# Sparse attention and MLP on one core: the softmax chain moved into one step, its normalization on ScalarE, its splitting on GpSimd

## The chip, the core and the metric

The kernel runs on one core of a Trainium2 chip. The core has five engines with a queue of instructions each, worked off strictly in order: TensorE (PE in the profile, with PEld for its weight loads), VectorE (DVE), ScalarE (ACT), GpSimd (POOL) and SyncE (SP), which here only issues DMAs. The engines wait for each other by semaphores. The metric is the device time of one execution in microseconds (us), lower is better. The kernel before takes 1460.08 us, the median of three runs from 1459.34 to 1460.13.

## The reference

Attention that keeps the 32 largest scores of each row, and then a two-layer MLP with a leaky ReLU, all in float32:

```python
# q, k, v: (8 batches, 8 heads, 576 rows, 64)
scores = q @ k.T / sqrt(64)                       # (8, 8, 576, 576)
kth = np.partition(scores, -32, axis=-1)[..., -32:-31]
scores = np.where(scores >= kth, scores, -1e9)
attn = np.exp(scores - scores.max(-1, keepdims=True))
attn = attn / (attn.sum(-1, keepdims=True) + 1e-9)
x = (attn @ v).transpose(0, 2, 1, 3).reshape(4608, 512)
h = x @ w_in                                      # w_in: 512 x 2048, in float64
out = np.maximum(0.01 * h, h) @ w_out             # w_out: 2048 x 512, in float64
```

## The kernel before, in words

**Units and steps.** The attention is cut into 144 *units*. Nearly every unit is 128 query rows of one pair of heads, so its scores are a tile of 128 partitions by 2 x 576 float32 (`s_sb`, held by `u.both` and `u.s`, five buffers); a few units per batch join the 64 left-over rows of two pairs. The main loop (L653 to L717) makes one pass per unit, called a *step* here. In step s, VectorE runs the top k of unit s, and the other engines work on units before and after it. All instructions are recorded in the order in which the loop writes them (`manual_schedule`), so the order on each engine's queue is that of the text.

**The chain of one unit**, with the step in which each part stands in the code before, for unit n:

- Step n-2 or so: `scores` (L218) on TensorE, for two units at once in every even step; four copies by ScalarE bring them from PSUM into `s_sb` (L242).
- Step n: `top_k` (L299) on VectorE, in four rounds, each of which is one `slot()` of the step: the halves of the row are paired by max and min (L306), and each round finds the eight largest (`MAX8`, L311) and strikes them out (`MATCH_REPLACE8`, L314).
- Step n+1: `limits` (L318) on GpSimd (three small instructions: `nleast`, then `nbias` twice), `mask` (L328, two ScalarE activations), `exponents` (L332, two more, which also give the sums), and `sums` (L336, `ze` on ScalarE), the last of them near the end of the step.
- Step n+2: `reciprocals` (L340, `rz` on VectorE), `normalize` (L344, two GpSimd multiplications of 128 x 576), and `transpose` (L347): ScalarE copies the upper and the lower 16 bits of all weights into two tiles (`split`, L354), SyncE writes both to DRAM (`apart`, L355) and brings them back through a transposing DMA (`wT`, L359).
- `values` (L635), attention times v on TensorE into a PSUM tile `wide` (L398, L410), for both units of a pair n, n+1 in the same step, and `keep_values` (L417), ScalarE's copies into `x` (L422). `values_at` (L525) says when: for a unit below 14 in the middle of step (n | 1) + 4, and from there on at the end of step (n | 1) + 3 (one step less for three units in `HURRIED`).

For units 14, 15, 23 and 31 (`HASTY`), `transpose_in_haste` (L361) takes the place of the DMAs: nine TensorE transposes into two PSUM tiles `wide`, and two ScalarE copies from there into `wT` (`keep_transposed`, L372).

**The MLP** goes over 19 chunks of tokens: two of 128, then seventeen of 256. A chunk becomes ready when the values of its last unit are kept: chunk 0 after units 0 to 3, chunk 1 after 4 to 7, chunk 2 after 8 to 15, and so on. TensorE does the hidden layer (`ph`, L467; L435 for the first two chunks) and the output layer (`pz`, L479); ScalarE applies the leaky ReLU (L473, L440) and copies the output (L488). `mlp_steps` (L501) puts a piece of this work at seven places in each step, and `slot_budget` (L553) sizes the pieces so that a chunk is used up when the next becomes ready. The last chunk is worked off after the loop (L718).

**What else stands in the order of the first steps.** Weights come in float64 and are turned to float32 first (`round_weights`, L115), until about 60 us. `score_early` (L573) computes the scores of twelve later units at the ends of steps 0 to 5 (4, 2, 1, 2, 1, 2 units): TensorE into `wide` and `narrow` PSUM tiles, two ScalarE copies per unit (L290), and a store to DRAM (`kept`). There are two PSUM tiles `wide`, shared by scores, early scores, transposes and values, and one `narrow`.

The heart of a step in the code before, where `old` is unit s-1 and `older` unit s-2:

```python
limits(old); weights_of(older)     # rz and the two multiplications of unit s-2
mask(old, 0); mask(old, 1)
exponents(old, 0)
transpose(older, lambda: mlp_steps(budget))
exponents(old, 1); sums(old)       # ze of unit s-1, used in step s+1
```

Of the kernel before, what the change touches and what calls it, by code (L numbers as in the profile page):

```python
# [13 lines left out]
AF = mybir.ActivationFunctionType  # L14
ALU = mybir.AluOpType

NKC = 5
# [3 lines left out]
def kernel(  # L21
# [13 lines left out]
    nc = tc.nc  # L35
# [4 lines left out]
    ROUNDS = TOPK // 8  # L40
# [258 lines left out]
    def top_k(u):  # L299

        u.tops = small.tile([P, 2, ROUNDS, 8], F32, name="tops")
        pairs = work.tile([P, 2, 2, HS], F32, name="pairs", bufs=1)
        for n, op in enumerate((ALU.max, ALU.min)):
            nc.vector.tensor_tensor(pairs[:, :, n, :], u.both[:, :, 0:HS], u.both[:, :, HS:S], op)  # L306
        for r in range(ROUNDS):
            rest = [pairs[:, i, 0, :] if r < ROUNDS // 2 else
                    pairs[:, i, :, :].rearrange("p n h -> p (n h)") for i in range(2)]
            for i in range(2):  # L310
                nc.vector.max(out=u.tops[:, i, r, :], in_=rest[i])  # L311
            if r + 1 < ROUNDS:
                for i in range(2):
                    nc.vector.match_replace(out=rest[i], in_to_replace=u.tops[:, i, r, :],  # L314
                                            in_values=rest[i], imm_value=LOWEST)
            yield

    def limits(u):  # L318

        largest, least_kept = u.tops[:, :, 0, 0], u.tops[:, :, ROUNDS - 1, 7]  # L320
        u.nleast = small.tile([P, 2], F32, name="nleast")
        u.nbias = small.tile([P, 2], F32, name="nbias")
        u.z = small.tile([P, 2], F32, name="z")
        nc.gpsimd.tensor_scalar(u.nleast, least_kept, -1.0, None, ALU.mult)  # L324
        nc.gpsimd.tensor_tensor(u.nbias, least_kept, largest, ALU.subtract)  # L325
        nc.gpsimd.tensor_scalar(u.nbias, u.nbias, SCALE, None, ALU.mult)

    def mask(u, i):  # L328

        nc.scalar.activation(u.s[i], u.s[i], AF.Prelu, bias=u.nleast[:, i:i + 1], scale=1.0, alpha=BELOW)  # L330
# [9 lines left out]
    def reciprocals(u):  # L340
        u.rz = small.tile([P, 2], F32, name="rz")
        nc.vector.reciprocal(u.rz, u.ze)  # L342

    def normalize(u, i):  # L344
        nc.gpsimd.tensor_scalar(u.s[i], u.s[i], u.rz[:, i:i + 1], None, ALU.mult)  # L345

    def transpose(u, between):  # L347


        pairs = u.both.rearrange("p i n -> p (i n)").bitcast(U16).rearrange("p (n h) -> p n h", h=2)  # L350
        apart = halves.tile([P, 2, 2 * S], U16, name="apart")
        for h in range(2):
            split = work.tile([P, 2 * S], U16, name="split", bufs=2)
            nc.scalar.copy(split, pairs[:, :, h])  # L354
            nc.sync.dma_start(apart[:, h, :], split)  # L355
            if h == 0:
                between()
        u.wT = work.tile([P, 2 * NKC - 1, P], F32, name="wT", bufs=3)
        nc.sync.dma_start_transpose(out=u.wT.bitcast(U16), in_=apart.rearrange("p h n -> (p h) n"))  # L359

    def transpose_in_haste(u):  # L361

        both = u.both.rearrange("p i n -> p (i n)")
        u.parts_T = []
        for c0, c1 in ((0, 8), (8, 2 * NKC - 1)):
            pt = ps_sc.tile([P, 2, 512], F32, name="wide", bufs=2)
            pt = pt.rearrange("p h (c n) -> p (h c) n", n=P)
            for c in range(c0, c1):
                nc.tensor.transpose(pt[:, c - c0, :], both[:, c * P:(c + 1) * P], ident)
            u.parts_T.append((c0, c1, pt))  # L370
# [18 lines left out]
    def weigh_whole(us, po, order):  # L389

        for m, c in enumerate(order):
            for side in range(2):
                k = slice(side * LEFT, (side + 1) * LEFT) if c == QUARTERS else slice(0, P)
                at = min(c, NKC - 1)
                for n, u in enumerate(us):
                    nc.tensor.matmul(  # L398
                        po[n * D:(n + 1) * D, side, 0:P],
                        v_of[u.pairs[0]][k, at, side, :],  # L400
                        u.wT[k, at + side * NKC if at + 1 < NKC else at, :],
                        start=(m == 0), stop=(m == NKC - 1),
                    )
# [112 lines left out]


    LAG = 3
    HURRY = 20
    HURRIED = (15, 23, 31)  # L520
    HASTY = (14, 15, 23, 31)
    UNHURRIED = 14
    MIDDLE, END = 0, 1

    def values_at(n):  # L525

        if n < UNHURRIED:
            return (n | 1) + LAG + 1, MIDDLE
        return (n | 1) + LAG - ((n | 1) in HURRIED), END

    steps = units

# [3 lines left out]
    def unit(n):  # L536
        return steps[n] if 0 <= n < len(steps) else None
# [26 lines left out]
    with tc.manual_schedule():  # L564
# [62 lines left out]
            if 0 <= n - len(jobs) + HP + 1 < HP:  # L627
                load_qk(n - len(jobs) + HP + 1)

        def weights_of(u):  # L630
            reciprocals(u)
            normalize(u, 0)
            normalize(u, 1)

        def values(*place):  # L635
            due = [u for n, u in enumerate(steps) if values_at(n) == place]
            if not due:
                return ()
            po = ps_sc.tile([P, 2, 512], F32, name="wide", bufs=2)
            if len(due[0].pairs) == 1:  # L640
                weigh_whole(due, po, FULL + [NKC - 1] if place[1] == MIDDLE else
                            [QUARTERS] + FULL if place[0] < HURRY else FULL + [QUARTERS])
                return [(due[0], po[:, :, 0:P])]
            for n, u in enumerate(due):
                weigh_left(u, po[:, :, n * LEFT:(n + 1) * LEFT])
            return [(u, po[:, :, n * LEFT:(n + 1) * LEFT]) for n, u in enumerate(due)]

        def keep(weighed, *place):
            for u, po in weighed:
                keep_values(u.pairs[0], po, u.b, u.q0)  # L650
            attended(*place)

        for s in range(len(steps) + LAG + 1):  # L653
            assert s < 7 or not to_keep
            cur, old, older, new = unit(s), unit(s - 1), unit(s - 2), ()
            if s % 2 == 0:
                new = [u for u in steps[s + 2:s + 4] if u]
            picks = top_k(cur) if cur else iter(())
            budget = slot_budget(s)

            def slot():
                next(picks, None)

            at_first = s < HURRY and s - 2 in HURRIED
            if at_first:
                weights_of(older)
            slot()
            if old:
                limits(old)
            late = s < HURRY and not {s - 1, s - 2} & set(HURRIED)  # L670
            if older and not late and not at_first:
                weights_of(older)
            mlp_steps(budget)
            if old:
                mask(old, 0)
                mask(old, 1)
            weighed = values(s, MIDDLE)
            at_once = s - 2 in HASTY or any(at == (s, MIDDLE) for at, _ in ready_at)
            if at_once:
                keep(weighed, s, MIDDLE)  # L680
            slot()
            if older and late:
                weights_of(older)
            if s - 2 in HASTY:
                transpose_in_haste(older)
            mlp_steps(budget)
            if old:
                exponents(old, 0)
            mlp_steps(budget)
            if older:  # L690
                keep_transposed(older) if s - 2 in HASTY else transpose(older, lambda: mlp_steps(budget))
            if not older or s - 2 in HASTY:
                mlp_steps(budget)
            if unit(s + 3) in early_units:
                fetch_scores(unit(s + 3))
            else:
                load_waiting()
            slot()
            slot()
            mlp_steps(budget)  # L700
            if old:
                exponents(old, 1)
                sums(old)
            mlp_steps(budget)
            if not at_once:
                keep(weighed, s, MIDDLE)
            if new and new[0] in early_units:
                new = ()
            if new and s < HURRY:
                scores(new)  # L710
            keep(values(s, END), s, END)
            if new and s >= HURRY:
# [65 lines left out]
```

## Time and profile before

| | us |
|---|---|
| median of three runs | 1460.08 |
| the profiled execution, its own time | 1464.25 |
| span of its profile | 1462.5 |
| TensorE busy in the span | 1399.0 (96%) |
| VectorE busy | 1313.9 (90%) |
| ScalarE busy | 1103.2 (75%) |
| GpSimd busy | 738.5 (50%) |

The profile is one execution. Its own time is 1.75 us above its span, which lies around it. A row of a group gives the engine, the operation, output and inputs, shapes and count, then the busy time, the mean of one in ns, and after the bar the idle time that the engine spent just before these instructions with what ended it. A row of the timeline gives start, duration, engine, line and operation. A matmul of float32 shows as two records. The clock that TensorE was granted stands as PEclk, as a share of full speed.

### The profile page before, as it was taken

How to read it: one execution, taken by the hardware profiler on the slowest of the kernel's cores; microseconds unless marked ns; L12 is line 12 of the kernel's file. 1: busy time of each engine (PE TensorE's matmuls, PEld its weight loads, DVE VectorE, ACT ScalarE, POOL GpSimd, SP SyncE). 2: the span in 40 equal slices, each digit the busy share in tenths (PEclk: the TensorE clock that was granted, in tenths of full speed). 3: DMA queues.
4: the chain of work that ended last, by engine and by line, in shares of the span. 5: the costliest groups of instructions: out<-in, count | busy, mean ns of one | idle time of the engine just before them, and what ended most of it. 6: DMA issues, size and time to landing. Idle time of an engine off the chain costs nothing.

```text
span 1462.5 us, 25892 instructions
## 1 busy us (share of the span) xinstructions
PE 1399.0 (96%) x8980; PEld 904.8 (62%) x8980; DVE 1313.9 (90%) x3401; ACT 1103.2 (75%) x1984; POOL 738.5 (50%) x744
## 2 busy tenths in 40 slices
PE   7847989999999999999999999999999999999998
PEld 2324547575666666666666666666666666666674
DVE  7998999999999999999999999999999999999500
ACT  8878877777787787777787878778778787778710
POOL 3245555555555555555555555555555555555500
PEclk9968999999999999999999999999999999999999
DMA  8967542657456555666655755666656665545610
GB/s 329 336 215 214 145 122 89 188 148 174 143 155 189 157 151 145 177 181 176 184 156 157 183 143 147 169 188 175 186 158 169 165 158 142 156 126 136 148 46 14
DMA packets 394995, 239.13 MB, mean 164 GB/s; under 512 B 334576, under 2 KB 336112, under 8 KB 392944
## 3 DMA queue, kind: packets, MB, share of 16 engines
q1 hardware_dynamic: 394864, 237.48, 57.8%
q8 instruction: 70, 1.15, 0.4%
q14 instruction: 61, 0.50, 0.1%
HBM read 55.77 MB, written 99.09 MB: 106 GB/s over the span
## 4 chain that ended last, share of the span: by engine, by line
PE 73%; DVE 13%; ACT 5%; DMA 5%; POOL 2%; issue 1%; SPq 0%; DVEq 0%; ACTq 0%; POOLq 0%
PE ph L467 27%; PE pz L479 27%; PE wide L398 9%; DVE tops L311 5%; PE wide L235 4%; DVE pairs L314 4%; PE narrow L235 3%; DMA wT<-apart 2%; ACT split L354 2%; POOL s_sb L345 1%; DVE pairs L306 1%; DMA apart<-split 1%; PE wide L410 1%; PE ph L435 1%; ACT s_sb L333 1%
## 5 line engine op out<-in xcount | busy, mean ns | idle before, releaser
L345 POOL TENSOR_SCALAR s_sb<-s_sb,rz 128x576 f32<-128x576 f32 x288 | 497.1, 1735 | 290.7 <-DVE rz L342 289.2
L311 DVE MAX8 tops<-pairs 128x8 f32<-128x288 f32 (+1 forms) x1152 | 637.7, 594 | 0.0
L479 PE MATMUL pz<-w_out,gT 128*128 128x512 f32 x1152 | 505.7, 595 | 0.5 <-ACT scale L440 0.5
L467 PE MATMUL ph<-x,w_in 128*128 128x256 f32 x2176 | 482.6, 381 | 0.0
L314 DVE MATCH_REPLACE8 pairs<-tops,pairs 128x288 f32<-128x288 f32 (+1 forms) x864 | 461.4, 541 | 0.0
L467 PEld LDWEIGHTS ph<-x,w_in 128*128 128x128 f32 x2176 | 409.5, 190 | 77.7 <-issue 23.5
L479 PEld LDWEIGHTS pz<-w_out,gT 128*128 128x128 f32 x1152 | 217.0, 190 | 265.4 <-issue 262.8
L354 ACT COPY split<-s_sb 128x1152 uint16<-128x1152 uint16 x280 | 310.4, 1149 | 83.8 <-POOL s_sb L345 82.4
L324 POOL TENSOR_SCALAR nleast<-tops 128x2 f32<-128x2 f32 x144 | 74.7, 519 | 308.3 <-DVE tops L311 308.3
L333 ACT ACTIVATE s_sb<-s_sb,nbias 128x576 f32<-128x576 f32 x288 | 222.2, 771 | 0.0
L306 DVE TENSOR_TENSOR pairs<-s_sb 128x576 f32<-128x576 f32 x288 | 206.9, 758 | 9.5
L330 ACT ACTIVATE s_sb<-s_sb,nleast 128x576 f32<-128x576 f32 x288 | 207.2, 772 | 1.6 <-POOL nleast L324 1.6
L398 PE MATMUL wide<-wT,vt 128*64 128x128 f32 (+1 forms) x2560 | 160.3, 282 | 15.1 <-DMA wT<-apart 10.0
L398 PEld LDWEIGHTS wide<-wT,vt 128*64 128x64 f32 (+1 forms) x2560 | 131.7, 137 | 64.8 <-issue 34.3
L473 ACT ACTIVATE gT<-ph 128x512 f32<-128x512 f32 x136 | 80.7, 593 | 60.3 <-PE ph L467 60.1
L422 ACT COPY x<-wide 128x128 f32<-128x128 f32 (+1 forms) x160 | 32.2, 260 | 108.3 <-PE wide L398 94.4
L242 ACT COPY s_sb<-wide 128x704 f32<-128x704 f32 x130 | 98.1, 755 | 8.9 <-PE wide L235 2.9
L325 POOL TENSOR_TENSOR nbias<-tops 128x2 f32<-128x2 f32 x144 | 95.2, 661 | 0.0
L235 PE MATMUL wide<-kt,qt 64*64 64x352 f32 x704 | 73.0, 477 | 1.0 <-ACT s_sb L257 0.7
L488 ACT COPY o_sb<-pz 128x512 f32<-128x512 f32 x36 | 21.0, 584 | 65.0 <-PE pz L479 65.0
L342 DVE RECIPROCAL rz<-ze 128x2 f32<-128x2 f32 x144 | 22.7, 158 | 48.8 <-ACT ze L338 48.5
L314 DVE MATCH_VALUE_LOAD pairs<-tops,pairs 128x8 f32 x864 | 65.0, 75 | 0.0
(70 smaller groups left out, 783.9 us busy)
## 6 DMA issues: line engine op xcount, KB each, us to landing
apart<-split SPq DMA_DIRECT2D x280, 288.0 KB, 2.1
raw<-in_weights_dram SPq DMA_DIRECT2D x15, 1024.0 KB, 7.2
vt<-in_vk_dram SPq DMA_DIRECT2D x32, 320.0 KB, 3.5
out_dram<-o_sb SPq DMA_DIRECT2D x36, 256.0 KB, 3.5
kept<-gT SPq DMA_DIRECT2D x12, 576.0 KB, 3.6
s_sb<-kept SPq DMA_DIRECT2D x12, 576.0 KB, 4.7
qt<-in_qT_dram SPq DMA_DIRECT2D x20, 288.0 KB, 3.3
kt<-in_kT_dram SPq DMA_DIRECT2D x20, 288.0 KB, 3.5
```

What stands on the lines that cost most here:

```text
L235: nc.tensor.matmul(to[r0:r0 + LEFT, i, :], qt[d, q0:q0 + LEFT], kt[d, k0:k1], start=True, stop=True)
L242: nc.scalar.copy(u.both[:, :, k0:k1], to)
L306: nc.vector.tensor_tensor(pairs[:, :, n, :], u.both[:, :, 0:HS], u.both[:, :, HS:S], op)
L311: nc.vector.max(out=u.tops[:, i, r, :], in_=rest[i])
L314: nc.vector.match_replace(out=rest[i], in_to_replace=u.tops[:, i, r, :], in_values=rest[i], imm_value=LOWEST)
L330: nc.scalar.activation(u.s[i], u.s[i], AF.Prelu, bias=u.nleast[:, i:i + 1], scale=1.0, alpha=BELOW)
L333: nc.scalar.activation(u.s[i], u.s[i], AF.Exp, bias=u.nbias[:, i:i + 1], scale=SCALE, accum_out=u.z[:, i:i + 1])
L345: nc.gpsimd.tensor_scalar(u.s[i], u.s[i], u.rz[:, i:i + 1], None, ALU.mult)
L354: nc.scalar.copy(split, pairs[:, :, h])
L398: nc.tensor.matmul(po[n * D:(n + 1) * D, side, 0:P], v_of[u.pairs[0]][k, at, side, :], u.wT[k, at + side * NKC if at + 1 < NKC else at, :] ...
L467: nc.tensor.matmul(ph[:, i, 0:n], w_in[c][:, f * P:(f + 1) * P], x[c][:, 0:n], start=(c == 0), stop=(c == HP - 1),)
L479: nc.tensor.matmul(pz[0:m, 0:DMODEL], gT[:, f, r0:r0 + m], w_out[f // 4][:, f % 4, :], start=(f == 0), stop=(f == NFC - 1),)
```

## The change

Normalization moves from GpSimd to ScalarE, the two splitting copies from ScalarE to GpSimd, and `nleast` from GpSimd to ScalarE. `reciprocals`, `normalize` and `transpose` of a unit move from step n+2 into step n+1, behind the exponents of the same step. The top k's third round is cut in two at a new `yield`, so that `rz` can stand between its search and its striking out in even steps and behind both in odd ones. The values of all units stand in the middle of step (n | 1) + 3, or one step earlier for units in `HASTY`, which is now 0 to 7, 14 and 15; the special orders for the hurried units go.

```diff
@@ top_k
                 nc.vector.max(out=u.tops[:, i, r, :], in_=rest[i])
+            if r == ROUNDS - 2:
+                yield
             if r + 1 < ROUNDS:
@@ limits
-        nc.gpsimd.tensor_scalar(u.nleast, least_kept, -1.0, None, ALU.mult)
+        nc.scalar.activation(u.nleast, least_kept, AF.Copy, bias=0.0, scale=-1.0)
@@ normalize
-        nc.gpsimd.tensor_scalar(u.s[i], u.s[i], u.rz[:, i:i + 1], None, ALU.mult)
+        nc.scalar.activation(u.s[i], u.s[i], AF.Copy, bias=0.0, scale=u.rz[:, i:i + 1])
@@ transpose
-            nc.scalar.copy(split, pairs[:, :, h])
+            nc.gpsimd.tensor_copy(split, pairs[:, :, h])
             nc.sync.dma_start(apart[:, h, :], split)
-            if h == 0:
-                between()
@@ values_at
-    HURRY = 20
-    HURRIED = (15, 23, 31)
-    HASTY = (14, 15, 23, 31)
-    UNHURRIED = 14
+    HASTY = (*range(8), 14, 15)
-        if n < UNHURRIED:
-            return (n | 1) + LAG + 1, MIDDLE
-        return (n | 1) + LAG - ((n | 1) in HURRIED), END
+        return (n | 1) + LAG - (n in HASTY), MIDDLE
@@ the loop over steps, as it stands after the change
+            slot()
+            if old:
+                limits(old)
+                mask(old, 0)
+            mlp_steps(budget)
+            if old:
+                mask(old, 1)
+            slot()
+            mlp_steps(budget)
+            if old:
+                exponents(old, 0)
+            weighed = values(s, MIDDLE)
+            if old:
+                exponents(old, 1)
+                sums(old)
+            keep(weighed, s, MIDDLE)
+            mlp_steps(budget)
+            slot()
+            if s % 2:
+                slot()
+            if old:
+                reciprocals(old)
+            mlp_steps(budget)
+            if old:
+                normalize(old, 0)
+                normalize(old, 1)
+            mlp_steps(budget)
+            slot()
+            slot()
...
+            if old:
+                if s - 1 in HASTY:
+                    transpose_in_haste(old)
+                    keep_transposed(old)
+                else:
+                    transpose(old)
             mlp_steps(budget)
+            if new:
                 scores(new)
             score_early(EARLY_SCORES.get(s, 0))
```

More of the change, by code (lines that the diff above doesn't have):

```diff
@@ L344, in normalize, with transpose @@
     def normalize(u, i):
-        nc.gpsimd.tensor_scalar(u.s[i], u.s[i], u.rz[:, i:i + 1], None, ALU.mult)
-    def transpose(u, between):
+        nc.scalar.activation(u.s[i], u.s[i], AF.Copy, bias=0.0, scale=u.rz[:, i:i + 1])
+    def transpose(u):
         pairs = u.both.rearrange("p i n -> p (i n)").bitcast(U16).rearrange("p (n h) -> p n h", h=2)
@@ L628 @@
                 load_qk(n - len(jobs) + HP + 1)
[L630 to L633, printed above, removed]
         def values(*place):
@@ L640, in values @@
             if len(due[0].pairs) == 1:
-                weigh_whole(due, po, FULL + [NKC - 1] if place[1] == MIDDLE else
-                            [QUARTERS] + FULL if place[0] < HURRY else FULL + [QUARTERS])
+                weigh_whole(due, po, FULL + [QUARTERS])
                 return [(due[0], po[:, :, 0:P])]
@@ L654 @@
             assert s < 7 or not to_keep
-            cur, old, older, new = unit(s), unit(s - 1), unit(s - 2), ()
+            cur, old, new = unit(s), unit(s - 1), ()
             if s % 2 == 0:
                 new = [u for u in steps[s + 2:s + 4] if u]
+            if new and new[0] in early_units:
+                new = ()
             picks = top_k(cur) if cur else iter(())
@@ L662, in slot @@
                 next(picks, None)
-            at_first = s < HURRY and s - 2 in HURRIED
-            if at_first:
-                weights_of(older)
             slot()
@@ L669 @@
                 limits(old)
-            late = s < HURRY and not {s - 1, s - 2} & set(HURRIED)
-            if older and not late and not at_first:
-                weights_of(older)
+                mask(old, 0)
             mlp_steps(budget)
             if old:
-                mask(old, 0)
                 mask(old, 1)
[L677 to L680, printed above, removed]
             slot()
[L682 to L685, printed above, removed]
             mlp_steps(budget)
@@ L688 @@
                 exponents(old, 0)
-            mlp_steps(budget)
[L690 to L693, printed above, removed]
+            weighed = values(s, MIDDLE)
[3 more added lines that the diff above has]
+            keep(weighed, s, MIDDLE)
+            mlp_steps(budget)
+            slot()
[10 more added lines that the diff above has]
+            slot()
             if unit(s + 3) in early_units:
@@ L697 @@
                 load_waiting()
-            slot()
-            slot()
-            mlp_steps(budget)
[L701 to L712, printed above, removed]
+            if old:
[4 more added lines that the diff above has]
+                    transpose(old)
+            mlp_steps(budget)
+            if new:
                 scores(new)
```

## The prediction

> **What bounds the kernel now.** I read the stretches of the span first, then the chain that ended last, then who waited for whom, then the timeline of the first steps. Busy time by stage (columns: stretch, PE, PEld, DVE, ACT, POOL with counts in brackets, PEclk, DMA share, GB/s):
>
> ```profile
> 61.00:154.00 93.00, 62.57 (x419) 35.62 (x418) 88.37 (x230) 71.12 (x129) 41.91 (x45) 0.80 0.71 225
> 154.00:230.00 76.00, 70.25 (x468) 37.98 (x467) 73.83 (x198) 60.26 (x116) 40.83 (x42) 0.98 0.44 117
> 230.00:1375.00 1145.00, 1133.76 (x7628) 760.98 (x7629) 1102.32 (x2885) 900.55 (x1655) 629.13 (x627) 1.00 0.60 161
> 1375.00:1463.00 88.00, 83.67 (x328) 50.31 (x326) 0.48 (x3) 17.41 (x31) 7.47 (x7) 1.00 0.18 53
> ```
>
> From 230 us on TensorE is busy 1133.8 of 1145 us; it lacks work only in the head (30.4 us idle from 61 to 154). VectorE is nearly as full. The chain, in order of time, shows where the full stretch begins and how it ends:
>
> ```profile
> 227.61 2.35 PE wide L398 x40
> 229.96 7.10 PE ph L467 x32
> ...
> 1403.38 27.82 PE ph L467 x128
> 1431.21 27.48 PE pz L479 x64
> ```
>
> 229.96 is the first matmul of chunk 2, the first large chunk. Its 16 intervals up to the start of the last chunk at 1403.38 are 73.3 us each, TensorE's work for eight steps. So the end is the start of chunk 2, plus 1173.4, plus 59.1. **Two questions decide: when does chunk 2 start, and does TensorE stay full behind it.** The waits say who could stop it (us in total, times, longest):
>
> ```profile
> DVE rz L342 <- ACT ze L338: 48.5, 45, 6.9
> ...
> PEld wide L398 <- DMA wT<-apart: 13.0, 12, 2.1
> ...
> PE wide L398 <- DMA wT<-apart: 10.0, 8, 1.9
> ```
>
> VectorE already waits for `ze`, though `rz` stands a step behind it; TensorE waits 10 us for late `wT`. The prices (start, duration, engine, line):
>
> ```profile
> 71.75 1.45 ACT L330 ACTIVATE s_sb<-s_sb,nleast 128x576 f32<-128x576 f32 x2
> 73.09 0.77 ACT L333 ACTIVATE s_sb<-s_sb,nbias 128x576 f32<-128x576 f32 x1
> ...
> 74.74 0.20 ACT L338 ACTIVATE ze<-z 128x2 f32<-128x2 f32 x1
> ```
> ```profile
> 217.19 4.44 POOL L345 TENSOR_SCALAR s_sb<-s_sb,rz 128x576 f32<-128x576 f32 x2 [3.74 <-DVE rz L342]
> ...
> 225.34 1.20 PE L369 MATMUL wide<-ident,s_sb 128*128 128x128 f32 x9
> ...
> 226.55 1.17 ACT L375 COPY wT<-wide 128x1024 f32<-128x1024 f32 x2
> ```
>
> Masks to `ze` is 71.75 to 74.94, 3.2 us; nine transposes 1.2; their copies 1.17. The pair on GpSimd took 4.44 there against 3.44 elsewhere, beside VectorE's two-input L306 (217.01 to 218.42): GpSimd loses about 1 us to it.
>
> **The change, engine by engine.** ScalarE: out go 280 splits (310.4 us in the group's row), in come 288 normalizations at the masks' 1.45 a pair (209), 144 `nleast` at `ze`'s 0.20 (29) and six more units of transposed copies (7): 65 us less, of no worth by itself. GpSimd: out go 497.1 and 74.7 us, in come 268 copies of 1152 two-byte elements. That copy is not in the trace; the nearest row is L131's strided two-byte copy, 1135 ns for 1024, so 1.28; the far end is L345's 1735 ns for 576, 3.5. I take 1.28 (same engine, operation and type). SyncE: 134 in place of 140 sets of three DMAs; other DMAs behind a set wait for its split as before. TensorE: 6 more units of 9 transposes in the idle head, 2 fewer (23 and 31) behind it, -2.4 us.
>
> **The head.** D(s) is the start of VectorE's step s: 61.32, 70.09, 78.90, 87.69 in the timeline, 8.75 to 8.8 apart; D(10) is 153.51, D(16) 206.81. After the change ScalarE's queue holds in each step, without a break, `nleast`, masks, exponents, `ze`, [`rz` on VectorE], normalization, [transposes on TensorE], copies of `wT`, in even steps four score copies, in steps 0 to 5 the early copies, and only then the next unit's `nleast`. And VectorE waits at `rz`. From one `rz` to the next therefore: 0.1 + 1.45 + 1.2 + 1.17 = 3.9, then the extras, then `nleast` to `ze` 3.65, `rz` 0.15: 7.7 plus extras. The extras: score copies 2.25 (90.26 to 92.50) plus 0.8 for TensorE's turn on the freed `wide`; one early unit 1.45 (two copies 1.2 and a turn), two 3.5. So odd steps with two early units cost 11.2, even ones with one 12.2, against VectorE's 8.75. The first `rz` is VectorE's: D(1) 70.1 + 7.25 = 77.35. Then 88.6, 100.8, 112.0, 124.2; step 5 to 6 takes 13.6 (0.4 for `x` copies and some 2 for L435's matmuls, 8 records of about 0.43, which come before the transposes), then 11.7 (score copies, `x`, one MLP copy of 0.6), 9.3 (`x`, two MLP copies), 11.4: `rz` of step 9 at 170.2. 1.4 us of VectorE's step follow it in odd steps, so D(10) is 171.6, **18 us later**. From there nothing is hasty until unit 14; at 8.8 a step D(16) is 224.4, 17.6 later. Then unit 15: `rz` at 231.5 (1 us late behind unit 14's copies), normalized 233.0, `wT` 235.4, score copies to 238.5, and the next unit's chain to `ze` 242.2, since `keep` now stands behind `sums`; `x` at 242.6 and chunk 2 at 242.7. Before it was 229.96: **+12.7**. The shorter chain gives back 4.9 of 17.6. Chunk 0 does start earlier (about 125 against 133.20), but its 15 us of work and chunk 1's are done in time either way.
>
> Ends: if the copies all hide, D(16) stays and chunk 2 starts 4.9 earlier; if each of the eight hasty steps costs 1.2 more, 22.3 later. I take +12.7: ScalarE's queue leaves nothing to overlap.
>
> The Trainium skill, TensorE: Matmul & The Clock Gate, section What's actually happening, speaks against the change here: after an idle window of about 3.4 us the array runs at half its clock. The trace agrees: the clock is 0.68 from 74 to 111 us, and early matmuls start 0.48 us apart from 92.55 to 93.51 against 0.24 from 64.80 to 65.29. By this rule the transposes of the head take 2.4 in place of 1.2, and the end would come some 9 us later than I say.
>
> **The middle.** In two steps TensorE has 18.3 us: 13.8 of MLP, 2.35 of values, 2 of scores. Three loops must fit. ScalarE alone: 2 x (0.2 + 1.45 + 1.65 + 0.2 + 1.45) + 0.43 + 2.25 + 1.5 of MLP = 14.1. The transposed weights of an odd unit: counted from TensorE's even step, `rz` 5.1, normalized 6.6 to 8.4 (MLP copies may stand before), split 2.6 plus 1 beside L306, DMAs 6.85 (split end 1119.05 to landing at 1125.9): 17 to 19 against a use at 20.3; that is more room than now. **The tight one** is GpSimd's queue: `nbias` of the next unit stands behind the split. From an odd step's `rz`: 0.1 + 1.45 + 2.6 + 1.0 + `nbias` 0.5 + exponents 1.65 + `ze` and hand-offs 0.5 = 7.8 to the even `rz`, and from there VectorE needs 2.7 + 7.2 + 0.3 = 10.2 to the odd one: 18.0. It fits by 0.3 us in two steps. So TensorE remains the bound and I cost the middle at 0, between -11.2 (all of TensorE's idle time there goes) and the loop's excess, 63 times what the pair of splits takes over 2.9: far end, 3.5 each, 63 x 4.1 = 260 us, which I don't weigh, since the far row is a float32 multiplication; with 1.75 each, 63 x 0.6 = 38.
>
> GPSIMD Engine Reference, section Elementwise — side-by-side cycle accounting, of the same skill gives 769 ns for 512 elements as a best case. Worked out from it, an estimate, a split would take 1.73 us, and the middle would lose those 38 us; the row of the trace says 0.
>
> **The tail.** After VectorE's last step TensorE has 16 pieces of MLP (some 15 us) before the last values, and the last unit's chain takes about 15: no change.
>
> **Sum.** +12.7 - 2.4 + 0 = +10.3. It is made against the profiled execution (1464.25, span 1462.5); that run is 4.2 above the median, which I take off from both sides alike: 1460.1 + 10.3 = **1470.4**.
>
> **The rivals.** (A) Faster: the head keeps VectorE's pace, since ScalarE's copies hide beside it; this holds if a hasty step's queue costs under 8.75 in place of 11 to 12. For it: ScalarE is busy only 71 of 93 us there. Against it: the order puts everything in line. Then -4.9 - 2.4 and about -8 of TensorE's 11.2 us of idle time: 1445. (B) GpSimd becomes the bound: the split's pair takes over 2.9 us, `nbias` is late and VectorE with it. For it: 4.44 against 3.44 beside L306, and `nleast` 783 ns in the median against 220 alone. Against: L131's row. With 38 us: 1508. (C) No difference: the head loses 8, and the middle wins 6 back, as the waits for `wT` (10 us) go: 1460.
>
> **How the numbers follow.** Forecast 0.50 (1463 to 1482: the head's +5.5 to +22.3, less 2.4, with the middle within 2), B 0.22, A 0.20, C 0.08. Faster than 1457.2 (0.2%, about what a measurement of this kernel can tell from no change) is A: 0.20; within it C: 0.08; slower 0.72. The range holds the forecast, C, and the nearer part of A and of B: 1446 to 1508, with some 0.1 left out at each side.
>
> **What will show it.** Right: D(10) near 171.6, VectorE waiting for `ze` by 1 to 3 us in each of steps 2 to 9, chunk 2 starting near 242.7, and 73.3 us per chunk behind it. Wrong: D(10) near 154 (A); a chunk's interval over 75 us with GpSimd's split over 1.45 us and `nbias` late (B); `wT` no longer waited for and intervals under 73 (C).

## The result and the profile after

The changed kernel takes 1592.04 us (median of four runs, 1589.77 to 1592.58), beside 1460.11 for the kernel before on the same chip: 1.0898 times as long, 95% interval 1.0879 to 1.0917. It is slower by 132 us where +10 was forecast; the direction held, the size did not. The profiled execution took 1592.58 with a span of 1590.8.

The stretches of the changed kernel, in the same columns as before (TensorE, its weight loads, VectorE, ScalarE, GpSimd, clock, DMA share, GB/s):

```profile
61.00:154.00 93.00, 63.68 (x394) 37.36 (x394) 66.51 (x176) 63.37 (x125) 8.83 (x14) 0.74 0.37 134
154.00:230.00 76.00, 70.38 (x429) 36.21 (x429) 69.34 (x170) 55.98 (x120) 21.23 (x26) 0.96 0.31 82
230.00:1375.00 1145.00, 1065.52 (x6935) 690.29 (x6933) 1110.03 (x2664) 753.33 (x1635) 400.77 (x459) 0.97 0.56 151
1375.00:1591.00 216.00, 207.08 (x1134) 134.94 (x1134) 127.37 (x305) 101.80 (x217) 49.81 (x58) 0.98 0.34 95
```

Two things are new. In the head VectorE is busy for only 66.5 of 93 us (88.4 before). In the long stretch TensorE is idle for 79.5 us (11.2 before), while VectorE is a little busier than before and does less: 2664 instructions where there were 2885. So VectorE's instructions have become longer on average. The chain that ended last, by engine and by line, on the page of the changed kernel:

```profile
DVE 67%; PE 13%; issue 9%; ACT 6%; DMA 3%; POOL 1%; SPq 1%; DVEq 0%; POOLq 0%; ACTq 0%
...
L356 POOL COPY split<-s_sb 128x1152 uint16<-128x1152 uint16 x268 | 363.7, 1385 | 852.6 <-ACT s_sb L347 852.6
...
L306 DVE TENSOR_TENSOR pairs<-s_sb 128x576 f32<-128x576 f32 x288 | 319.1, 1148 | 5.0
```

The chain, 73% TensorE before, now runs through VectorE. One group explains it: L306, the max and min of the two halves of the row, takes 1148 ns instead of 758, 112 us more in all. By the tile `pairs`, with shortest, median and longest duration, this is L306 in the kernel before:

```profile
L306 DVE TENSOR_TENSOR pairs<-s_sb x288: 737/753/787, 61.3 to 1367.1; 128x576 f32<-128x576 f32 x144
```

and this in the changed kernel, together with the one-input MAX8 of the same tile:

```profile
L311 DVE MAX8 tops<-pairs x1152: 432/592/754, 61.8 to 1509.7; 128x8 f32<-128x288 f32 x96, 128x8 f32<-128x576 f32 x96
...
L306 DVE TENSOR_TENSOR pairs<-s_sb x288: 743/759/1711, 60.5 to 1502.4; 128x576 f32<-128x576 f32 x144
```

L306 is either what it was or about a microsecond longer; MAX8, which reads one tile, is untouched. The timeline of two steps in the middle (start, duration, engine, line) shows what the long ones have beside them:

```profile
805.20 0.14 DVE L344 RECIPROCAL rz<-ze 128x2 f32<-128x2 f32 x1
...
806.88 2.23 POOL L356 COPY split<-s_sb 128x1152 uint16<-128x1152 uint16 x2 [4.61 <-ACT s_sb L347]
...
808.15 2.24 DVE L306 TENSOR_TENSOR pairs<-s_sb 128x576 f32<-128x576 f32 x2
...
817.74 2.37 DVE L306 TENSOR_TENSOR pairs<-s_sb 128x576 f32<-128x576 f32 x2
...
817.93 3.19 POOL L356 COPY split<-s_sb 128x1152 uint16<-128x1152 uint16 x2 [7.47 <-ACT s_sb L347]
```

A pair of L306 takes 1.43 us when it is alone. At 808.15 GpSimd's second copy is under way; it ends at 806.88 + 2.23 = 809.11, and the pair of L306 is longer by 0.81. At 817.74 L306 begins first; the first copy now waits for it, and the second L306 waits for that copy: the pair takes 0.94 more, the copies 0.96 more. VectorE's own work for two steps is about 17.55 us (8.77 to 8.81 a step in the first steps of the kernel before, 8.77 a step in run 5 below, where the two do not meet); 17.55 + 0.81 + 0.94 = 19.30. The chain, in order of time, has that period:

```profile
808.15 1.63 DVE pairs L306 x2
827.45 1.63 DVE pairs L306 x2
846.76 1.64 DVE pairs L306 x2
```

TensorE needed 18.3 us for two steps before; in the new order it needs 18.55 (74.2 us per chunk in runs 2, 5 and 8, where it is the bound). VectorE, which stood a little below it, now stands 0.75 us above it.

In such steps VectorE waits for nothing: from 260 us on it waits at `rz` only five times, 4.8 to 9.8 us each. The second loss is in the waits of the changed kernel (us in total, times, longest):

```profile
ACT s_sb L335 <- POOL nbias L328: 125.2, 71, 2.2
...
DVE rz L344 <- ACT ze L340: 76.2, 17, 9.8
...
PE wide L410 <- DMA vt<-in_vk_dram: 46.7, 8, 10.9
```

TensorE waited 0.3 us for `vt` (the rows of v) before and waits 46.7 now, most of it in four halts of 8.5 to 10.9 us near 310, 665, 1022 and 1379 us. The first of them in the timeline:

```profile
304.01 2.56 SPq L359 DMA_TRANSPOSE wT<-apart  x1
...
306.62 0.58 SPq L180 DMA_DIRECT2D vt<-in_vk_dram  x1
...
310.00 2.40 PE L410 MATMUL wide<-wT,vt 128*64 128x64 f32 x38 [10.80 <-DMA vt<-in_vk_dram]
312.44 0.56 ACT L422 COPY x<-wide 128x64 f32<-128x64 f32 x4 [8.27 <-PE wide L410]
...
324.00 0.17 DVE L344 RECIPROCAL rz<-ze 128x2 f32<-128x2 f32 x1 [8.50 <-ACT ze L340]
```

SyncE issues the load of `vt` only behind the transposing DMA of that step, 0.05 us after the DMA's issue ends, and the values that need it come half a step earlier than they used to. Then `x` is late on ScalarE, then the next unit's `ze`, and VectorE waits 8.5 us as well.

**The sum, as the prediction made it.** Chunk 2 starts at 256.3 (before: 229.9): +26.4. Its sixteen intervals take 1275.4 in place of 1173.4: +102.0. What follows the start of the last chunk takes 59.1 (59.2). Together +128.3, which is the difference of the two spans.

### The profile page after: what moved, and what is told of

The parts are those of the page before. It is cut to its first block, busy times and chain, and to the rows that moved or that the text cites. A ratio compares the mean times of both kernels' runs of the same rounds, so it can differ in the third digit from the quotient of the medians.

```text
span 1590.8 us, 25920 instructions
## 1 busy us (share of the span) xinstructions
PE 1455.0 (91%) x9032; PEld 918.6 (58%) x9034; DVE 1423.0 (89%) x3401; ACT 1028.8 (65%) x2148; POOL 499.8 (31%) x580
## 4 chain that ended last, share of the span: by engine, by line
DVE 67%; PE 13%; issue 9%; ACT 6%; DMA 3%; POOL 1%; SPq 1%; DVEq 0%; POOLq 0%; ACTq 0%
DVE tops L311 31%; DVE pairs L316 24%; DVE pairs L306 9%; PE pz L479 5%; PE ph L467 2%; ACT s_sb L335 1%; PE wide L398 1%; POOL split L356 1%; PE wide L369 1%; PE ph L435 1%; ACT s_sb L347 1%; DMA raw<-in_weights_dram 1%; ACT s_sb L242 1%; DMA apart<-split 1%; PE wide L286 1%
## 5 line engine op out<-in xcount | busy, mean ns | idle before, releaser
L356 POOL COPY split<-s_sb 128x1152 uint16<-128x1152 uint16 x268 | 363.7, 1385 | 852.6 <-ACT s_sb L347 852.6
L479 PE MATMUL pz<-w_out,gT 128*128 128x512 f32 x1152 | 515.5, 601 | 1.3 <-ACT gT L473 1.1
L467 PE MATMUL ph<-x,w_in 128*128 128x256 f32 x2176 | 495.1, 384 | 6.9 <-ACT gT L473 5.8
L347 ACT ACTIVATE s_sb<-s_sb,rz 128x576 f32<-128x576 f32 x288 | 207.5, 768 | 242.6 <-DVE rz L344 242.6
L306 DVE TENSOR_TENSOR pairs<-s_sb 128x576 f32<-128x576 f32 x288 | 319.1, 1148 | 5.0
L398 PE MATMUL wide<-wT,vt 128*64 128x128 f32 (+1 forms) x2560 | 165.3, 287 | 18.6 <-DMA wT<-apart 17.6
L398 PEld LDWEIGHTS wide<-wT,vt 128*64 128x64 f32 (+1 forms) x2560 | 133.5, 140 | 71.3 <-issue 44.9
L327 POOL TENSOR_TENSOR nbias<-tops 128x2 f32<-128x2 f32 x144 | 63.7, 443 | 118.1 <-DVE tops L311 106.0
L344 DVE RECIPROCAL rz<-ze 128x2 f32<-128x2 f32 x144 | 21.2, 147 | 76.2 <-ACT ze L340 76.2
L410 PE MATMUL wide<-wT,vt 128*64 128x64 f32 x640 | 27.7, 252 | 46.7 <-DMA vt<-in_vk_dram 46.7
L242 ACT COPY s_sb<-narrow 128x448 f32<-128x448 f32 x130 | 63.0, 539 | 2.4 <-PE narrow L235 2.2
L316 DVE MATCH_VALUE_LOAD pairs<-tops,pairs 128x8 f32 x864 | 61.5, 71 | 0.0
```

The source lines that it names most:

```text
L242: nc.scalar.copy(u.both[:, :, k0:k1], to)
L347: nc.scalar.activation(u.s[i], u.s[i], AF.Copy, bias=0.0, scale=u.rz[:, i:i + 1])
L356: nc.gpsimd.tensor_copy(split, pairs[:, :, h])
L398: nc.tensor.matmul(po[n * D:(n + 1) * D, side, 0:P], v_of[u.pairs[0]][k, at, side, :], u.wT[k, at + side * NKC if at + 1 < NKC else at, :] ...
L467: nc.tensor.matmul(ph[:, i, 0:n], w_in[c][:, f * P:(f + 1) * P], x[c][:, 0:n], start=(c == 0), stop=(c == HP - 1),)
L479: nc.tensor.matmul(pz[0:m, 0:DMODEL], gT[:, f, r0:r0 + m], w_out[f // 4][:, f % 4, :], start=(f == 0), stop=(f == NFC - 1),)
```

## The experiments

All times are medians; ratios, with their 95% intervals, are against the kernel before on the same chip. The runs were made on four chips, on which the kernel before takes 1460.5 to 1464.2 us in the median, so differences in us between runs are good to some 4 us. "Intervals" are the sixteen from the start of chunk 2 to the start of the last chunk. Diffs are against the changed kernel unless another is named. Theory 1: VectorE has become the bound, since L306 and GpSimd's copies shut each other out. Theory 2: GpSimd's queue, with `nbias` late behind the split (rival B). Beside both stand two losses of their own, the late load of `vt` and the slow head.

**1. `nbias` on VectorE.** This was to take the 125 us of ScalarE's waits for GpSimd's `nbias` out of the way of the split.

```diff
-        nc.gpsimd.tensor_tensor(u.nbias, least_kept, largest, ALU.subtract)
-        nc.gpsimd.tensor_scalar(u.nbias, u.nbias, SCALE, None, ALU.mult)
+        nc.vector.tensor_tensor(u.nbias, least_kept, largest, ALU.subtract)
+        nc.vector.tensor_scalar(u.nbias, u.nbias, SCALE, None, ALU.mult)
```

> The kernel after, with the two small nbias instructions on VectorE in place of GpSimd, so that they no longer stand behind the splits. Theory 1 (VectorE is the bound in the middle because L306 runs at 1.15 us in place of 0.75 beside GpSimd's splitting copies): L306 stays at 1.10 to 1.15 us, ScalarE's 125 us of waiting for nbias goes, and the time does not fall; it rises by 10 to 50 us, since each step of VectorE carries two more instructions. Theory 2 (the queue: nbias behind the split makes exponents and rz late): the time falls by 20 to 60 us and VectorE's 76 us of waiting for ze falls by half.

Measured: 1624.45 us, 1.1127 [1.1110, 1.1145], 32 more than the changed kernel. L306 stays at 1158 ns. The run did not do what was meant: on VectorE's queue `nbias` stands behind the first round of the next top k and comes later than before, and ScalarE's wait for it nearly doubles in place of going.

```profile
ACT s_sb L335 <- DVE nbias L328: 235.8, 125, 2.6
...
DVE rz L344 <- ACT ze L340: 65.0, 16, 9.3
```

It speaks against theory 2 all the same. With `nbias` later still, VectorE waits for `ze` no longer than before (65.0 us in 16 times, 76.2 in 17). And the two small instructions, 147 and 170 ns, lengthen each step by what they take: the usual interval of 77.2 becomes 79.6, 0.3 us for each of its eight steps, and 34 of their 46 us show in the intervals. VectorE is the bound, and the late `nbias`, visible though it is, does not reach it.

**2. The split back on ScalarE.**

```diff
-            nc.gpsimd.tensor_copy(split, pairs[:, :, h])
+            nc.scalar.copy(split, pairs[:, :, h])
```

> The kernel after, with the two splitting copies back on ScalarE. Theory 1: L306 returns to 0.75 us (207 us in total), two steps of VectorE shrink from 19.3 to some 17.6 us, and ScalarE, which gains 4.4 us in two steps (14.1 to 18.5), becomes the bound with TensorE at 18.5; time 1592 - 16 x 3 = 1535 to 1550, with the vt waits (47 us) and the head's delay left. Theory 2 expects a gain as well, but L306 to stay above 1 us.

Measured: 1528.21 us, 1.0459 [1.0442, 1.0477]: 64 less. L306 by its tile:

```profile
L306 DVE TENSOR_TENSOR pairs<-s_sb x288: 746/754/786, 60.8 to 1435.5; 128x576 f32<-128x576 f32 x144
```

The intervals without a `vt` halt fall from about 77 to 71.9 to 74.2, some 3 us or four times 0.75. All sixteen lose 62 us, but 21 of these are `vt` halts that became shorter (46.7 to 26.0 us); some 41 are left for L306. ScalarE is busy for 1313 us and is not the bound even so: the chain that ended last is TensorE for 82%.

**3. `vt` loaded earlier in the step**, just behind `keep` and so ahead of the split's DMAs on SyncE.

```diff
             keep(weighed, s, MIDDLE)
+            load_more(s)
...
-            load_more(s)
```

> The kernel after, with load_more (the loads of v, q and k) put behind keep in the middle of the step in place of its end, ahead of the step's split, apart and transposing DMAs on SyncE's queue. If the four large waits of L410 for vt (10.8 us at 310 us and the like, 46.7 us in all) set the end, they fall under 6 us in total and the time falls by 30 to 40 us, to 1552 to 1562. If VectorE's steps alone set it, the waits go and the time stays within 5 us of 1592.

Measured: 1561.69 us, 1.0694 [1.0678, 1.0710]: 30 less. The wait of the changed kernel is all but gone:

```profile
PE wide L410 <- DMA vt<-in_vk_dram: 4.4, 4, 1.3
```

The intervals of 90.8, 89.0 and 89.5 become 76 to 79, and all sixteen together lose 33.6 us; the wait for `wT` rises from 17.6 to 27.7, and the loads now stand ahead of those transfers.

**4. Transposes on TensorE for units 14 and 15 alone**, so that units 0 to 7 go by DMA as they did before.

```diff
-    HASTY = (*range(8), 14, 15)
+    HASTY = (14, 15)
```

> The kernel after, with units 0 to 7 transposed by DMA again (HASTY is 14 and 15 only, their values one step later). If ScalarE's and TensorE's train of transposes in steps 1 to 8 makes the head late, D(10) falls from 179.0 to 160 to 168 and chunk 2's first matmul from 256 to 240 to 248, and the time falls by 8 to 16 us. If the head is late for another reason (top k slowed by GpSimd, early scores), D(10) stays above 174 and the time within 4 us; with splits on GpSimd in the head too, L306 there rises from 0.72 to over 1.

Measured: 1571.75 us, 1.0763 [1.0745, 1.0781]: 20 less, more than expected. VectorE's step 10 begins at 159.4 (179.0 in the changed kernel, 153.5 before), chunk 2 at 234.8 (256.3). So the eight units that were transposed on TensorE first, with their values a step earlier, made up 21 of the 26 us lost in the head, although in their place splits now meet L306 there (2.2 to 2.4 us a pair).

**5. The split one step later, behind the next `limits`**, so that GpSimd's copies follow L306 and stand ahead of nothing urgent.

```diff
+            if unit(s - 2) and s - 2 not in HASTY:
+                transpose(unit(s - 2))
             if old:
                 mask(old, 0)
...
-                else:
-                    transpose(old)
```

> The kernel after, with nothing changed but the place of the splits on GpSimd's queue (and of the DMAs behind them): they are issued behind the next step's nbias, which itself runs beside L306, so that they start when L306 is over. Theory 1 (a splitting copy and a two-input L306 shut each other out, and that sets the middle): L306 falls from 1.15 to 0.75 or 0.80 us, two steps of VectorE from 19.3 to 17.6 to 17.9 us, TensorE sets the pace again at 18.3 to 18.6, and the time falls by 16 x 3 to 4 = 48 to 62 us, to 1530 to 1545, although wT lands some 2 us later and TensorE's waits for it rise above 17.6 us. If VectorE was slow for another reason (rz inside the top k, the third round cut in two), L306 falls but the time stays above 1575.

Measured: 1501.43 us, 1.0265 [1.0245, 1.0285]: 91 less, with the same instructions on the same engines. The groups of this kernel:

```profile
L356 POOL COPY split<-s_sb 128x1152 uint16<-128x1152 uint16 x268 | 298.9, 1143 | 5.1 <-ACT s_sb L347 5.1
...
L306 DVE TENSOR_TENSOR pairs<-s_sb 128x576 f32<-128x576 f32 x288 | 205.5, 754 | 4.9
```

Both sides are at their price alone. ScalarE's waits for `nbias` go as well in this order, so the run by itself does not part theory 1 from theory 2; run 1 does, and the long stretches in which the changed kernel's VectorE waits for nothing. VectorE's steps take 8.77 us again though `rz` stands inside the top k, so that isn't the cause either. The intervals lose 88.7 us, which includes the halts for `vt`: that wait falls to 1.9. I expected `wT` to be later; its wait fell to 5.0.

**6. The kernel before, with its split on GpSimd and nothing else changed.**

```diff
-            nc.scalar.copy(split, pairs[:, :, h])
+            nc.gpsimd.tensor_copy(split, pairs[:, :, h])
```

> The kernel before, with the two splitting copies on GpSimd and nothing else changed. GpSimd then normalizes (3.44 us) and splits (2.3 us) from about 3 us to 9 us into a step of VectorE, so that part of the splits meets the next L306. Theory 1: L306 rises from 0.72 us to 0.80 to 1.05, and the time to 1465 to 1510. If the slow L306 belongs to the new order of the chain and not to GpSimd's copies: L306 stays at 0.72 to 0.76 and the time within 6 us of 1460.

Measured: 1465.30 us, 1.0013 [1.0003, 1.0022]. Two effects cancel. In the head, two steps of this kernel's timeline:

```profile
86.39 2.76 POOL L354 COPY split<-s_sb 128x1152 uint16<-128x1152 uint16 x2
86.89 2.86 DVE L306 TENSOR_TENSOR pairs<-s_sb 128x576 f32<-128x576 f32 x2
...
96.59 2.76 POOL L354 COPY split<-s_sb 128x1152 uint16<-128x1152 uint16 x2
97.17 2.79 DVE L306 TENSOR_TENSOR pairs<-s_sb 128x576 f32<-128x576 f32 x2
```

Here the copies fall on L306: 2.86 in place of 1.43 for the pair, VectorE's steps 10.2 us apart, chunk 2 at 244.8, 15 us late. Behind it the two hardly meet (one pair of 124 is longer), and the intervals take 1159.3, 14 us less than before.

**7. A slower instruction in the copy's place.** If the copy holds VectorE off until it ends, one of three times the length must hold it off for three times as long.

```diff
-            nc.gpsimd.tensor_copy(split, pairs[:, :, h])
+            nc.gpsimd.tensor_scalar(split, pairs[:, :, h], 1.0, None, ALU.mult)
```

> The kernel after, with the splits on GpSimd as a multiplication by 1 (the kind of instruction that normalized before) in place of a copy, to the same values. If only copies shut VectorE out, as the kernel before suggests, where a normalization beside L306 took 1 us longer and L306 did not: L306 returns to 0.72 to 0.80. If any GpSimd instruction on a large tile does: L306 stays above 1.0. The split itself costs 1.4 us if it runs like the copy, and then the time goes to 1530 to 1550 in the first case; up to 3.5 us if it runs like the normalization, and then GpSimd's queue makes nbias late and the time goes above 1650.

Measured: 2009.39 us, 1.3734 [1.3713, 1.3756]. The group of the split in this kernel:

```profile
L356 POOL TENSOR_SCALAR split<-s_sb 128x1152 uint16<-128x1152 uint16 x268 | 894.2, 3353 | 772.5 <-ACT s_sb L347 751.0 <-ACT nleast L326 21.6
```

and its tile `pairs`:

```profile
L311 DVE MAX8 tops<-pairs x1152: 433/592/754, 62.0 to 1917.1; 128x8 f32<-128x288 f32 x96, 128x8 f32<-128x576 f32 x96
...
L306 DVE TENSOR_TENSOR pairs<-s_sb x288: 745/2722/3449, 60.6 to 1907.1; 128x576 f32<-128x576 f32 x144
```

L306 now takes up to 3.45 us; MAX8 still takes what it did. It is not the copy as such, and it is not shared speed: the second to come waits for the end of the first. The ends show it. Where the multiplication was under way when an L306 began, by 0.3 to 1.2 us, L306 ended 0.36 to 0.38 us after it in all 190 cases. In the changed kernel L306 ended 0.61 us after the copy that was under way in 130 of 131 cases, and where L306 was under way when a copy began, the copy ended 1.00 us after L306 in all 135.

**8. The three mends together**: runs 3, 4 and 5 in one kernel.

> The kernel after, with the three causes taken away together: the splits behind the next step's nbias, load_more behind keep, and only units 14 and 15 transposed on TensorE. Theory 1 with its two side causes, if they add up: L306 at 0.75 to 0.80 us, L410's waits for vt under 6 us, chunk 2's first matmul at 226 to 236, and 1592 - 55 - 31 - 20 = 1475 to 1495; if TensorE is full behind chunk 2 as before, 1455 to 1470. If a further cause is left, it stays above 1500.

Measured: 1478.12 us, 1.0104 [1.0087, 1.0121]: 114 of the 132 us come back. Against the kernel before, its span is 13.1 longer: 1.6 in the start of chunk 2 (231.5), 11.8 in the intervals (1185.2), -0.3 in the tail. Of the intervals the first stands out with 88.2 (before 73.6): it spans nine of VectorE's steps, since units 22 and 23 are no longer hurried. The kernel before has its interval of nine steps too, the third, which takes 80.4 there and 74.2 here; so 8.4 of the 11.8 lie in these two. Others take 74.2 where the kernel before takes about 73.3. For those, the weight loads' waits of this kernel show

```profile
PEld wide L235 <- issue: 33.1, 60, 0.8
```

against 4.8 us in 8 times before: scores and values stand apart in the step now, each between pieces of the MLP, and most such entries of the scores now wait about half a microsecond.

**9. The kernel before, with the splits of units from 18 on moved to GpSimd.** Run 6 without its loss in the head. The diff is against the kernel before.

```diff
-            nc.scalar.copy(split, pairs[:, :, h])
+            (nc.gpsimd.tensor_copy if steps.index(u) >= 18 else nc.scalar.copy)(split, pairs[:, :, h])
```

> The kernel before, with the splits of units 18 to 143 on GpSimd and those of the first 18 on ScalarE as they were. With all splits on GpSimd the 16 intervals from chunk 2 to the last chunk took 1159.3 us against 1173.4, but chunk 2 began at 244.8 against 229.9, since in the first steps GpSimd's splits met L306. If the two are separate: chunk 2 stays at 229 to 232, the intervals sum to 1158 to 1163, and the time is 1445 to 1452, under the kernel before. If the middle was only shorter because work had piled up behind the late head: the intervals sum to 1170 or more and the time stays at 1457 to 1464.

Measured: 1448.33 us, 0.9897 [0.9882, 0.9911]: 15 us faster than the kernel before, and the fastest of all. In the timeline of its middle the split follows the normalization on GpSimd at once and is done as L306 begins:

```profile
799.77 3.45 POOL L345 TENSOR_SCALAR s_sb<-s_sb,rz 128x576 f32<-128x576 f32 x2 [1.41 <-DVE rz L342]
803.28 2.23 POOL L354 COPY split<-s_sb 128x1152 uint16<-128x1152 uint16 x2
805.37 1.43 DVE L306 TENSOR_TENSOR pairs<-s_sb 128x576 f32<-128x576 f32 x2
```

Its intervals sum to 1157.9 (1173.4), and its waits for the transposed weights and for `ze` fall:

```profile
DVE rz L342 <- ACT ze L338: 29.2, 31, 3.1
...
PE wide L398 <- DMA wT<-apart: 2.0, 2, 1.3
```

TensorE is busy for 1142.7 of 1145 us from 230 us on, 8.9 more than before. The other 6 or so lie in the values themselves: the matmuls of L398 are busy for 154.1 us where they took 160.3. Why they run shorter, no run shows.

**10. The eighth kernel, with units 15, 23 and 31 hurried again.**

```diff
-    HASTY = (14, 15)
+    HURRIED = (15, 23, 31)
+    HASTY = (14, 15, 23, 31)
...
-        return (n | 1) + LAG - (n in HASTY), MIDDLE
+        return (n | 1) + LAG - ((n | 1) in HURRIED), MIDDLE
```

> The three causes taken away as in the 1478 us kernel, and the values of units 22, 23, 30 and 31 one step earlier, with 23 and 31 transposed on TensorE, as the kernel before has them. There the first interval, from chunk 2 to chunk 3, took 88.2 us, since it spans nine steps of VectorE in place of eight while TensorE has no other work. If that is the rest: the first interval falls to 74 to 80, a later one rises to 78 to 82, and the time falls by 8 to 13 us, to 1465 to 1470; the intervals of 74.2 stay, so it does not reach 1460. If the rest lies elsewhere, the time stays within 4 us of 1478.

Measured: 1478.59 us, 1.0110 [1.0091, 1.0128], no gain. The first interval falls from 88.2 to 76.2, but the third rises from 74.2 to 82.3, several others rise by 0.7 to 2.0, and the sum stays at 1186. The ninth step is moved, not saved.

**11. The eighth kernel, with the scores right behind the values**, so that TensorE leaves the MLP once where it left it twice.

```diff
             keep(weighed, s, MIDDLE)
+            if new:
+                scores(new)
             load_more(s)
...
-            if new:
-                scores(new)
```

> The 1478 us kernel with the scores of the next two units issued right behind the values and their copies, in place of near the end of the step. There TensorE showed as full in the intervals of 74.2 us, against 72.8 in the kernel at 1448, which has values and scores side by side, and its weight loads for the scores waited 56 times for half a us on its own issue (30.1 us), against 3 times (1.0 us) in the kernel before. If each separate entry into scores costs TensorE: those waits fall under 5 us, the intervals of 74.2 fall to 72.8 to 73.3, and the time falls by 12 to 20 us, to 1458 to 1466. If the 1.4 us an interval come from elsewhere: intervals stay at 74, time within 4 us of 1478. Against it stands that ScalarE's score copies (2.25 us) come before the normalization, so that wT lands later; waits for wT above 30 us would eat the gain.

Measured: 1475.52 us, 1.0077 [1.0055, 1.0099], 2.6 less than the eighth; much more was expected. The intervals of 74.2 do become 72.8 (the entries, then, cost 1.4 us per chunk), but chunk 2 starts 4.3 later, and the wait for `wT` rises from 11.5 to 18.1. Of the 11 us that still separate this kernel from the one before, I can name the place, the head and the first interval, but no cause that a run has shown.

## Why the prediction was wrong

**The middle, "I cost the middle at 0": wrong by 102 us, the largest part of them by one step, the price of the split beside L306.** The prediction saw the collision: it read 4.44 against 3.44 us for GpSimd's pair beside "VectorE's two-input L306", concluded that "GpSimd loses about 1 us to it", and put VectorE's loss at nothing. That row is the only one of the kernel before in which a normalization meets L306, and it does read so: both L306 took their usual 0.74 and 0.75 us, although the second began 0.48 us after the normalization. The copies behave otherwise. By the prediction's own numbers the split starts 1.6 us after `rz`, L306 1.4 us after it in odd steps, and in even steps the copies are under way when L306 comes; in the trace VectorE then loses 0.94 and 0.81 us, in every step.

Runs 5 and 7 show the mutual hold. Its price lies between the 41 us of run 2 and the 57 by which the intervals of run 8 are shorter than those of run 3, with `vt` early in both (run 8 also has run 4's edit, which by itself moves the intervals by 1 us). The 102 us can be told as 33.6 for `vt` (run 3), 56.6 more for the place of the split (run 8) and 11.8 that run 8 leaves; in another order the shares differ, since the split's place alone (run 5) takes the `vt` halts along.

The Trainium skill, SBUF — State Buffer, section Who interferes with whom, states the rule: a VectorE instruction with two SBUF inputs contends with a GpSimd instruction that reads SBUF, whichever is issued first keeps the shared port pair for its whole length, and a VectorE instruction with at most one SBUF input isn't affected, outside the modes that use both ports. The runs agree for the splits (L306 up to 1711 ns beside a copy of 1.14 us, up to 3449 beside a multiplication of 3.13; MAX8 over 288 elements 442 ns beside a copy and 443 elsewhere). The row at 217.19 us does not: there the second L306 began after the normalization and lost nothing, and why, no run shows. The prediction didn't weigh this page; it is the rule that spoke against the change.

**Rival B, GpSimd's queue: its condition came true, and no price of it was found.** ScalarE did wait for `nbias` 71 times, 125 us in all. But VectorE waits at `rz` only 17 times, and in run 1, with `nbias` later still, no more. The loop of 18.0 us was worked out against TensorE's 18.3, while VectorE's own 19.3 had become the larger number.

**"Other DMAs behind a set wait for its split as before": wrong by about 30 us.** The other DMAs do wait behind the set, as was said; but the set stands elsewhere in the step, and what needs `vt` comes earlier. The edit was costed at nothing without asking who uses the load, and when. Run 3 gave 30 us back.

**The head: right in mechanism, too small.** D(10) came at 179.0 where 171.6 was said, and VectorE did wait for `ze` in each of the steps 2 to 9, though by 3.6 to 6.0 us up to step 6 and by 0.9 to 1.9 behind, where 1 to 3 was said. The delay had come by step 5 (its `rz` at 132.25, where 124.2 was said), with a granted clock of 0.60 from 77 to 132 us; behind it, at 1.00 from 132 to 178, the steps took what the sum says. The missing 7.4 us are near the estimate by the Trainium skill, TensorE: Matmul & The Clock Gate, section What's actually happening, which the prediction gave beside its sum, some 9 us for a cold array. No run sets the clock apart, so this cause is argued, not shown. The chain of the changed kernel has the transposes at 1.98 for eight, not at 1.2 for nine:

```profile
76.72 0.79 ACT s_sb L347
77.55 1.98 PE wide L369 x8
79.56 1.02 ACT wT L375
```

From step 10 to step 16 came 60.0 us, not 52.8: 4.6 of the difference are longer pairs of L306, which splits had begun to meet, and 2.6 are two waits for `ze`. So D(16) was 239.0 (224.4 said), and with 17.3 to chunk 2 (18.3 said) its start is 256.3, not 242.7: +26.4 against +12.7.

**The first interval was missed.** That it would span nine steps of VectorE follows from the hurried units' going; the sum had 73.3 for it. With the other losses mended it is 14 to 15 us longer than before (runs 5 and 8), and the third, which had the ninth step before, 6 us shorter; run 10 shows that hurrying the units again only moves this.

**What held.** The tail (59.1). The price of a split alone: 1.28 taken, 1.14 measured. The room for the transposed weights held only in the order of run 5, where they are waited for 5.0 us, half of before; in the changed kernel itself it was 17.6. That ScalarE's relief is "of no worth by itself" was not tested in the new order; in the old one run 9, which takes 252 us off ScalarE from 230 us on, gains 15 us. The separate entry of values and scores, 1.4 us per chunk, is not in the prediction.

## What to carry to other kernels

Before an instruction is moved to GpSimd, list the VectorE instructions that read two tiles in SBUF and ask, for each, which of the two begins first: in these runs the second waited for the split to end, or the split for it, and where VectorE is nearly full this lands on the end. The same copies cost some 41 to 57 us in one place of the step, nothing in another, and in the kernel before, where they fill GpSimd's gap ahead of L306, they win 15. A single row that shows a collision prices only that instruction in that order, and a load that "waits as before" must be checked against its user, which may have moved.

## What the runs showed of the hardware

- VectorE's L306 (two inputs of 128 x 576 float32) takes 0.75 us alone and up to 1.71 when a GpSimd copy of 1.14 us has begun before it, up to 3.45 when it is a multiplication of 3.13. The one normalization that met L306 (217.19 us, kernel before) did not lengthen it. MAX8 and MATCH_REPLACE8 kept their durations in every run.
- GpSimd copies 1152 two-byte elements per partition in 1.14 us, no slower than ScalarE did (1149 ns), but multiplies the same elements by 1.0 in 3.13 undisturbed.
- An early transpose on TensorE costs more than its count says: 1.98 us for eight at 77.55 us, with a granted clock of 0.60 from 77 to 132 us, where nine took 1.20 at 225 us in the kernel before.
